# Attention in two bursts of three score blocks a turn, with PSUM banks shared out anew

## The chip, the cores and the metric

One core of a Trainium2 chip runs the whole program. The metric is the device time of one execution in microseconds, the median of the runs shown. Engines are named as the profile names them: PE (TensorE, matmuls), DVE (VectorE), ACT (ScalarE), POOL (GpSimd) and SP, which issues DMAs. Each takes its instructions in the order in which they stand in its queue.

## What is computed

Sigmoid attention for 4 batches of 12 heads (448 tokens, 64 wide), then two layers on its output:

```python
def _attn_ref(q, k, v):
    scores = scale * np.matmul(q, k.transpose(0, 1, 3, 2)) - np.log(S)
    attn = 1.0 / (1.0 + np.exp(-scores))
    return np.matmul(attn, v)

def _moe_ref(x, w_in, w_spatial, b_spatial, w_out):
    h = np.maximum(x @ w_in, 0.0)
    u, v = h[..., :512], h[..., 512:]
    v_n = (v - mean(v)) / np.sqrt(var(v) + 1e-06)
    v_s = np.einsum('ts,bsd->btd', w_spatial, v_n) + b_spatial[None, :, None]
    return (u * v_s) @ w_out

def _moe2_ref(x, g_ln, w_ch1, w_ch2):
    xn = normalised(x) * g_ln
    return x + np.maximum(xn @ w_ch1, 0.0) @ w_ch2
```

## The kernel before

Most products are made of three matmuls on operands split in two parts (`mm3`, lines 265 to 268: high x high, high x low, low x high). Attention fills the first 226 of 1063 us; the rest of the kernel is untouched by the change.

Attention works on pairs of heads, 24 in all, numbered p. A **turn** of the main loop (from line 815 on) handles pairs p and p+1; turn t has p = 2t. A pair's 448 key rows are three blocks of 128 (`scores`, six matmuls a block, line 416, two at a time on the two row halves of the array) and a rest of 64, which `scores_rest` (line 429) does for two pairs at once. Each block of scores goes into a double PSUM bank, from which ACT's sigmoid (line 403) writes SBUF. `sums` (line 456) multiplies a pair's three blocks with its values v, and `sums_rest` (line 443) adds the rest; `x_end` then writes the pair's columns of x, by a copy on ACT (line 303) and a subtraction on DVE (line 304). Where this text says **rests**, it means `scores_rest` of this turn's pairs, `sums_rest` of the turn before, and one `x_end`.

Ahead of a pair's scores its q and k are loaded by SP (four DMAs, lines 379 and 380) into rings of three, and split by `qk_split`: two casts on DVE (lines 395, 398) and, from pair 2 on, two subtractions on POOL (lines 399, 400). The split parts lie in rings of two, so the cast for pair p+2 waits for the scores of pair p.

Beside attention the first layer begins. Its weight w_in comes in eight **chunks**: chunks 0 to 3 for `hv`, 4 to 7 for `hu`. A chunk passes four steps: *load* (SP, line 277, 768 KB), *scale* (POOL, line 284), *bits* (three operations on DVE, lines 293, 294, 297) and *split* (a copy on ACT, line 303, and a subtraction on DVE, line 304). Raw chunks lie in a ring of two, so the load of chunk 3 waits for the bits of chunk 1. `W_IN_PLAN` says at which point of which turn a step is issued: "3A" is turn 3 behind its first burst of scores. The products (`hv`, a group of 18 matmuls with 512 columns; `hu`, 18 with 448) come from a generator that `Stream.run` advances by a budget of microseconds, `4 * BG_US` = 9.2 a turn; it yields None when an input isn't settled, that is when it wasn't written at least `LAG` = 1 step back. A group of 18 accumulates in one PSUM bank, is passed through Relu on ACT (lines 521, 550) and stored.

A turn before: the rests, scores of two blocks, sums of pair p-1, two blocks, sums of pair p, two blocks, products. The eight PSUM banks are four for two double banks (scores), two for products (`ps1`) and two for sums (`psa`). The engines' queues follow the program's order; nothing is reordered.

Of the kernel before, what the change touches and what calls it, by code (L numbers as in the profile page):

```python
# [16 lines left out]
P = 128  # L17
# [4 lines left out]
KC = DM // P  # L22
# [19 lines left out]
LAG = 1  # L42
# [16 lines left out]
    "5B": ["split 7"],  # L59
# [135 lines left out]
class Stream:  # L195
# [21 lines left out]
def sigmoid_attention_gmlp_mlp(ctx: ExitStack, tc, q, k, v, w_in, w_sp, w_out, g_ln, w1, w2, out):  # L217
# [6 lines left out]
    ps_a = ctx.enter_context(tc.tile_pool(name="ps_a", bufs=2, space=bass.MemoryType.PSUM))  # L224
# [25 lines left out]
    def psa():  # L250
        return ps_a.tile([P, 512], F32, tag="psa", name="psa")

    singles = [lambda: ps_1.tile([P, 512], F32, tag="ps1", name="ps1")]

    def ps1():
        singles.append(singles.pop(0))
        return singles[-1]()

    def ps2():
        return ps_s.tile([P, 2, 512], F32, tag="ps2", name="ps2")  # L260
# [12 lines left out]
    vu = dict(v=Ring(F, DH, 2), u=Ring(F, S, 2))  # L273
# [32 lines left out]
    class Chunk:  # L306


        def __init__(self, src, place):
            self.src, self.place, self.ready = src, place, None  # L310
# [42 lines left out]
    rv = Ring(F, 512, 4)  # L353
    af_r = Ring(F, 2 * S, 5)
# [7 lines left out]
    x_done = {}  # L362
# [71 lines left out]
    def sums_rest(p):  # L434
# [3 lines left out]
        pairs[p + 1]["ps"] = psa()  # L438
# [25 lines left out]
    def x_end(p):  # L464
# [6 lines left out]
        x_done[b, hp] = now[0]  # L471
# [32 lines left out]
    def hv(b):  # L504
# [4 lines left out]
        for c in range(NB2 // 2, NB2) if b % 2 else range(NB2 // 2):  # L509
            ps = ps1()  # L510
            cols = slice(c * P, (c + 1) * P)
            for kc in range(KC):
                while not settled(x_done.get((b, kc)), 1) or not all(
                    settled(t.ready) for t in wv_chunks[: -(-(kc + 1) * DH // WC)]
                ):
                    yield None
# [3 lines left out]
            vf = vu["v"].next().ap(DH)  # L520
# [6 lines left out]
            yield 3 * 0.216  # L527
# [8 lines left out]
    def hu(b):  # L536
# [278 lines left out]
    for p in range(0, n_pairs, 2):  # L815
        if p:
            rests(p)
        scores((p, 0), (p, 1))
        w_in_step(f"{p // 2}A")
# [3 lines left out]
        else:  # L823
            rests(p)
# [24 lines left out]
    now[0] += 1  # L849
# [4 lines left out]
    for r in a_rings:  # L854
        r.free()
# [158 lines left out]
```

## Time and profile before

| | us |
|---|---|
| three runs | 1064.35, 1065.24, 1065.28 (median 1065.24) |
| the profiled execution | 1065.46 |
| its span, first to last instruction | 1063.3 |
| PE busy in the span | 1055.5 (99%) |
| PEld, DVE, ACT, POOL busy | 914.0, 550.7, 298.2, 118.1 |

The durations below come from the profiled execution. In a timeline each line is a run of like instructions: its start, the time to the end of the last of them, engine, line, operation, and how many; what stands in brackets is idle time before it and what ended it. Matmuls overlap, so the pace of a run is read from the distance of starts. Where a matmul of two parts is one instruction in the program, the trace may count two (sums: six matmuls, x12).

### The profile page before, as it was taken

The page shows a single profiled execution, that of the slowest core. Times are in us where ns is not written, and L with a number is a line of the kernel's source. Part 1 is how long each engine was busy: PE and PEld are TensorE (multiplying, and loading weights), DVE is VectorE, ACT ScalarE, POOL GpSimd, SP SyncE. Part 2 cuts the span into 40 slices and gives each one's busy share as a digit, 9 for nine tenths or more (in the row PEclk, how much of TensorE's full clock was granted, in tenths as well). Part 3 has the DMA queues.
Part 4 walks back from the last instruction along what each step waited for, and adds up shares of the span by engine and source line. Part 5 has one row for each costly group of instructions (what it writes and reads, how often), then busy time and mean ns, then how long its engine had stood idle before and what let it go on. Part 6 is the DMA issues. An engine that isn't in the chain of part 4 may idle for free.

```text
span 1063.3 us, 14008 instructions
## 1 busy us (share of the span) xinstructions
PE 1055.5 (99%) x5812; PEld 914.0 (86%) x5812; DVE 550.7 (52%) x789; ACT 298.2 (28%) x445; POOL 118.1 (11%) x104
## 2 busy tenths in 40 slices
PE   8999999999999999999999999999999999999998
PEld 5556666679999999999989899998999898999988
DVE  3764131146757755463646465555646364645533
ACT  5754444434523421111212121211112121112100
POOL 4553211122134400000000000000000000000000
PEclk9999999999999999999999999999999999999999
DMA  8853336254301111010202111110202020111013
GB/s 219 239 171 101 126 110 178 82 193 130 138 1 59 62 60 60 25 65 30 90 30 73 47 60 60 60 60 30 72 18 89 30 90 30 60 60 60 1 60 149
DMA packets 31951, 87.15 MB, mean 82 GB/s; under 512 B 7568, under 2 KB 16016, under 8 KB 31760
## 3 DMA queue, kind: packets, MB, share of 16 engines
q1 hardware_dynamic: 29808, 78.23, 22.9%
q0 software_dynamic: 1600, 7.34, 2.0%
q8 instruction: 46, 0.75, 0.3%
q10 hardware_dynamic: 480, 0.69, 0.2%
q14 instruction: 17, 0.14, 0.0%
HBM read 73.38 MB, written 12.86 MB: 81 GB/s over the span
## 4 chain that ended last, share of the span: by engine, by line
PE 96%; DMA 1%; DVE 1%; issue 0%; POOL 0%; ACT 0%; ACTq 0%; DVEq 0%; SPq 0%
PE ps L266 22%; PE ps L268 22%; PE ps L267 22%; PE psa L268 6%; PE psa L267 6%; PE psa L266 6%; PE psa L456 5%; PE ps L416 4%; PE ps L429 1%; PE psa L443 1%; DMA f_all<-in_k 1%; PE psa L654 0%; PE ps L654 0%; DMA f_all<-in_w_in 0%; DMA f_all<-in_q 0%; DVE f_all L294 0%
## 5 line engine op out<-in xcount | busy, mean ns | idle before, releaser
L266 PE MATMUL ps<-r_all 128*128 128x384 f32 (+2 forms) x1250 | 435.8, 349 | 0.0
L268 PE MATMUL ps<-r_all 128*128 128x384 f32 (+2 forms) x1250 | 433.8, 347 | 0.0
L267 PE MATMUL ps<-r_all 128*128 128x384 f32 (+2 forms) x1250 | 433.6, 347 | 0.0
L266 PEld LDWEIGHTS ps<-r_all 128*128 128x128 f32 x1250 | 235.1, 188 | 17.8 <-issue 3.8
L267 PEld LDWEIGHTS ps<-r_all 128*128 128x128 f32 x1250 | 235.1, 188 | 14.1
L268 PEld LDWEIGHTS ps<-r_all 128*128 128x128 f32 x1250 | 234.9, 188 | 12.9
L709 DVE TENSOR_TENSOR f_all<-ps,f_all 128x768 f32<-128x768 f32 x168 | 160.4, 955 | 163.1 <-PE ps L268 163.1
L268 PE MATMUL psa<-r_all 128*128 128x512 f32 (+3 forms) x338 | 123.6, 366 | 0.0
L267 PE MATMUL psa<-r_all 128*128 128x512 f32 (+3 forms) x338 | 123.4, 365 | 0.0
L266 PE MATMUL psa<-r_all 128*128 128x512 f32 (+3 forms) x338 | 123.0, 364 | 0.0
L691 ACT ACTIVATE r_all<-psa 128x512 fp32r<-128x512 f32 (+1 forms) x48 | 26.0, 541 | 276.5 <-PE psa L268 276.5
L303 ACT CAST r_all<-f_all 128x768 fp32r<-128x768 f32 x60 | 49.9, 834 | 172.3 <-DVE f_all L297 138.6
L403 ACT ACTIVATE f_all<-ps,bias_s 128x896 f32<-128x896 f32 x84 | 80.8, 1005 | 44.6 <-PE ps L416 23.4
L692 DVE SCALAR_TENSOR_TENSOR r_all<-ps,r_all 128x512 fp32r<-128x512 f32 (+1 forms) x48 | 29.9, 623 | 90.6 <-ACT r_all L691 90.6
L268 PEld LDWEIGHTS psa<-r_all 128*128 128x128 f32 x338 | 63.7, 188 | 9.6
L304 DVE TENSOR_TENSOR r_all<-f_all,r_all 128x768 fp32r<-128x768 f32 x60 | 59.6, 994 | 23.6 <-ACT r_all L303 23.6
L267 PEld LDWEIGHTS psa<-r_all 128*128 128x128 f32 x338 | 63.6, 188 | 8.8
L266 PEld LDWEIGHTS psa<-r_all 128*128 128x128 f32 x338 | 63.7, 188 | 8.6
L416 PEld LDWEIGHTS ps<-r_all 64*128 64x128 f32 x432 | 37.7, 184 | 28.5 <-issue 17.4
L294 DVE SCALAR_TENSOR_TENSOR f_all<-f_all 128x768 uint32<-128x768 uint32 x60 | 60.6, 1009 | 2.1
L304 DVE TENSOR_TENSOR r_all<-psa,r_all 128x448 fp32r<-128x448 f32 (+1 forms) x38 | 22.6, 595 | 74.0 <-ACT r_all L303 73.9
L456 PE MATMUL psa<-f_all 128*64 128x448 f32 x288 | 59.6, 548 | 1.1 <-DVE r_all L304 1.1
(85 smaller groups left out, 673.8 us busy)
## 6 DMA issues: line engine op xcount, KB each, us to landing
f_all<-in_w SPq DMA_DIRECT2D x48, 768.0 KB, 4.2
f_all<-in_v SPq DMA_DIRECT2D x24, 256.0 KB, 3.8
f_all<-in_w_in SPq DMA_DIRECT2D x8, 768.0 KB, 5.2
f_all<-in_k SPq DMA_DIRECT2D x45, 112.0 KB, 3.6
f_all<-in_q SPq DMA_DIRECT2D x45, 112.0 KB, 3.7
out_y<-f_all SPq DMA_DIRECT2D x13, 384.0 KB, 2.3
vscr<-f_all SPq DMA_DIRECT2D x14, 256.0 KB, 2.0
uscr<-f_all SPq DMA_DIRECT2D x16, 224.0 KB, 1.9
```

The source lines that it names most:

```text
L266: nc.tensor.matmul(ps, lh, rh, start=first, stop=False)
L267: nc.tensor.matmul(ps, lh, rl, start=False, stop=False)
L268: nc.tensor.matmul(ps, ll, rh, start=False, stop=last)
L294: nc.vector.scalar_tensor_tensor(bits, low, 29, bits, op0=ALU.logical_shift_right, op1=ALU.bitwise_or)
L303: nc.scalar.copy(hi, x)
L304: eng.tensor_sub(lo, x, hi)
L403: nc.scalar.activation(af, ps[:, :, :S], AF.Sigmoid, bias=bias_s, scale=1.0 / math.sqrt(D))
L416: nc.tensor.matmul(ps[:, j, :S], a[w][rows, kc], a[x][rows], start=(i == 0), stop=(i == 2))
L456: nc.tensor.matmul(a["ps"][rows, :S], a["v"][:, 4 * j + c], af[:, j], start=(p % 2 == 0 and c == 0), stop=(p % 2 == 1 and c == 2),)
L691: nc.scalar.activation(hh[:, f], ps[:, :n], AF.Relu)
L692: nc.vector.scalar_tensor_tensor(hl[:, f], ps[:, :n], 0.0, hh[:, f], op0=ALU.max, op1=ALU.subtract)
L709: nc.vector.tensor_add(y[:, hs], ps, y[:, hs])
```

## The change

Scores go out in two bursts of three blocks a turn, pair by pair, where three bursts of two stood. A third double bank joins them (`ps_x`, for the time of attention); sums and products now share the two banks of `ps1`, and `psa` is gone. For that, products are issued in whole groups (`Stream.run` stops only where the yielded cost is not positive), and a group is begun only when all of its batch's x and all chunks of its weight have been issued; that they were issued a step back is no longer asked (`LAG` is gone). A turn is now: the rests, three blocks, sums of pair p-1, products, three blocks, sums of pair p. The casts for pair p+2 stand behind the first burst, the values of pair p+1 are loaded in the turn of pair p (a ring of three in place of four), and `W_IN_PLAN` names its points anew (A, B, C, D: behind the first burst, ahead of products, behind them, at the turn's end).

```diff
 W_IN_PLAN = {
-    "0B": ["scale 0"],
-    "1A": ["bits 0", "scale 1"],
-    "1B": ["split 0", "bits 1", "load 2"],
+    "0D": ["scale 0"],
+    "1A": ["bits 0"],
+    "1B": ["load 2", "scale 1"],
+    "1D": ["split 0", "bits 1"],
     "2A": ["split 1", "load 3", "scale 2"],
-    "2B": ["bits 2", "scale 3"],
+    "2D": ["bits 2", "scale 3"],
     "3A": ["split 2", "bits 3", "load 4"],
-    "3B": ["split 3", "load 5", "scale 4"],
-    "3C": ["bits 4", "scale 5"],
-    "4A": ["split 4", "bits 5", "load 6"],
-    "4B": ["split 5", "load 7", "scale 6"],
-    "4C": ["bits 6", "scale 7"],
-    "5A": ["split 6", "bits 7"],
-    "5B": ["split 7"],
+    "3B": ["split 3", "load 5", "scale 4", "bits 4"],
+    "3C": ["split 4", "load 6", "scale 5"],
+    "3D": ["bits 5"],
+    "4A": ["split 5", "load 7", "scale 6"],
+    "4B": ["bits 6", "scale 7"],
+    "4C": ["split 6"],
+    "4D": ["bits 7"],
+    "5A": ["split 7"],
 }
...
     def run(self, us):
         self.owed += us
-        while self.owed > 0 and not self.done:
-            try:
-                cost = next(self.gen)
-            except StopIteration:
+        cost = 0.0
+        while not self.done and (self.owed > 0 or cost > 0):
+            cost = next(self.gen, None)
+            if cost is None:
                 self.done = True
-                return
-            if cost is None:
+            elif cost == 0:
                 self.owed = 0.0
-                return
-            self.owed -= cost
+            else:
+                self.owed -= abs(cost)
...
-    ps_a = ctx.enter_context(tc.tile_pool(name="ps_a", bufs=2, space=bass.MemoryType.PSUM))
...
+    ps_x = att.enter_context(tc.tile_pool(name="ps_x", bufs=1, space=bass.MemoryType.PSUM))
+    doubles += [double(ps_s), double(ps_x)]
...
-    rv = Ring(F, 512, 4)
-    af_r = Ring(F, 2 * S, 5)
+    rv = Ring(F, 512, 3)
+    af_r = Ring(F, 2 * S, 6)
...
-        pairs[p + 1]["ps"] = psa()
+        pairs[p + 1]["ps"] = ps1()
...
         for c in range(NB2 // 2, NB2) if b % 2 else range(NB2 // 2):
+            while (b, KC - 1) not in x_done or not wv_chunks[-1].ready:
+                yield 0
             ps = ps1()
             cols = slice(c * P, (c + 1) * P)
             for kc in range(KC):
-                while not settled(x_done.get((b, kc)), 1) or not all(
-                    settled(t.ready) for t in wv_chunks[: -(-(kc + 1) * DH // WC)]
-                ):
-                    yield None
...
     for p in range(0, n_pairs, 2):
+        turn = p // 2
         if p:
             rests(p)
-        scores((p, 0), (p, 1))
-        w_in_step(f"{p // 2}A")
+        scores((p, 0), (p, 1), (p, 2))
+        if not p:
+            rests(p)
+        qk_split(p + 2)
+        w_in_step(f"{turn}A")
         if p:
             sums(p - 1)
             x_end(p - 1)
-        else:
-            rests(p)
         qk_load(p + 3)
         if not p:
             wv_chunks[1].load()
-        beside()
         qk_load(p + 4)
+        if p:
+            pv_load(p + 1)
         pv_load(p + 2)
-        pv_load(p + 3)
...
-        scores((p, 2), (p + 1, 0))
-        beside()
+        beside(f"{turn}B")
+        bg.run(4 * BG_US)
+        beside(f"{turn}C")
+        scores((p + 1, 0), (p + 1, 1), (p + 1, 2))
+        qk_split(p + 3)
+        beside("")
         sums(p)
-        qk_split(p + 2)
-        w_in_step(f"{p // 2}B")
-        beside()
-        scores((p + 1, 1), (p + 1, 2))
-        qk_split(p + 3)
-        beside()
-        bg.run(4 * BG_US)
-        w_in_step(f"{p // 2}C")
+        beside(f"{turn}D")
```

The order on three engines, before and now. A name with a number (ps_444) is one PSUM tile; "x6" counts like instructions; r_all and f_all are the two SBUF arenas; lines of the changed kernel are some two to five higher (416 is 418, 429 is 431, 443 is 445, 456 is 458, 403 is 405, 303 is 308, 304 is 309, 395 and 398 are 397 and 400, 266 to 268 are 271 to 273).

PE in turn 3, from the rests to the first products, before:

```order
L429 MATMUL ps_431<-f_all 64x448 x4
L443 MATMUL psa<-f_all 64x448 x4
L416 MATMUL ps_444<-r_all 128x448 x6
L416 MATMUL ps_452<-r_all 128x448 x6
L456 MATMUL psa<-f_all 64x448 x6
L416 MATMUL ps_484<-r_all 128x448 x6
L416 MATMUL ps_492<-r_all 128x448 x6
L456 MATMUL psa<-f_all 64x448 x6
L416 MATMUL ps_515<-r_all 128x448 x6
L416 MATMUL ps_523<-r_all 128x448 x6
L266 MATMUL ps_215<-r_all 128x512
L267 MATMUL ps_215<-r_all 128x512
```

and now:

```order
L431 MATMUL ps_420<-f_all 64x448 x4
L445 MATMUL ps_409<-f_all 64x448 x2
L445 MATMUL ps_426<-f_all 64x448 x2
L418 MATMUL ps_433<-r_all 128x448 x6
L418 MATMUL ps_441<-r_all 128x448 x6
L418 MATMUL ps_449<-r_all 128x448 x6
L458 MATMUL ps_426<-f_all 64x448 x6
L271 MATMUL ps_492<-r_all 128x512
L272 MATMUL ps_492<-r_all 128x512
L273 MATMUL ps_492<-r_all 128x512
```

The three bursts of two blocks are two of three, and products stand between them, right behind the sums; in the changed kernel 54 product matmuls stand there in a row, where 45 stood at the turn's end before. Over all turns, products stand in ten turns before (turns 1, 2, 3 and 5 to 11) and in eight now (3 and 5 to 11).

DVE in turn 1, from a pair's end to the bits of chunk 1, before:

```order
L304 TENSOR_TENSOR r_all<-psa,r_all 128x448
L293 TENSOR_SCALAR f_all<-f_all 128x768
L294 SCALAR_TENSOR_TENSOR f_all<-f_all 128x768
L297 SCALAR_TENSOR_TENSOR f_all<-f_all 128x768
L304 TENSOR_TENSOR r_all<-psa,r_all 128x448
L395 CAST r_all<-f_all 128x384
L398 CAST r_all<-f_all 128x448
L304 TENSOR_TENSOR r_all<-f_all,r_all 128x768
L293 TENSOR_SCALAR f_all<-f_all 128x768
L294 SCALAR_TENSOR_TENSOR f_all<-f_all 128x768
L297 SCALAR_TENSOR_TENSOR f_all<-f_all 128x768
```

and now, from the casts for pair 4:

```order
L397 CAST r_all<-f_all 128x384
L400 CAST r_all<-f_all 128x448
L298 TENSOR_SCALAR f_all<-f_all 128x768
L299 SCALAR_TENSOR_TENSOR f_all<-f_all 128x768
L302 SCALAR_TENSOR_TENSOR f_all<-f_all 128x768
L309 TENSOR_TENSOR r_all<-ps_220,r_all 128x448
L397 CAST r_all<-f_all 128x384
L400 CAST r_all<-f_all 128x448
L309 TENSOR_TENSOR r_all<-f_all,r_all 128x768
L298 TENSOR_SCALAR f_all<-f_all 128x768
L299 SCALAR_TENSOR_TENSOR f_all<-f_all 128x768
L302 SCALAR_TENSOR_TENSOR f_all<-f_all 128x768
```

The first three operations of lines 293 to 297 (now 298 to 302) are the bits of chunk 0, the second three those of chunk 1. Both moved back: the casts of a pair stand ahead of each, and the second also stands behind the casts for pair 5, which wait for the turn's second burst.

ACT in turn 4, from the first block's sigmoid to the sigmoid of the next rests, before:

```order
L403 ACTIVATE f_all<-ps_614,bias_s 128x896
L403 ACTIVATE f_all<-ps_622,bias_s 128x896
L303 CAST r_all<-f_all 128x768
L303 CAST r_all<-psa 128x448
L403 ACTIVATE f_all<-ps_654,bias_s 128x896
L403 ACTIVATE f_all<-ps_662,bias_s 128x896
L303 CAST r_all<-f_all 128x768
L403 ACTIVATE f_all<-ps_685,bias_s 128x896
L403 ACTIVATE f_all<-ps_693,bias_s 128x896
L403 ACTIVATE f_all<-ps_709,bias_s 128x896
```

and now:

```order
L405 ACTIVATE f_all<-ps_619,bias_s 128x896
L405 ACTIVATE f_all<-ps_627,bias_s 128x896
L405 ACTIVATE f_all<-ps_635,bias_s 128x896
L308 CAST r_all<-f_all 128x768
L308 CAST r_all<-ps_612 128x448
L308 CAST r_all<-f_all 128x768
L405 ACTIVATE f_all<-ps_675,bias_s 128x896
L405 ACTIVATE f_all<-ps_683,bias_s 128x896
L405 ACTIVATE f_all<-ps_691,bias_s 128x896
L405 ACTIVATE f_all<-ps_713,bias_s 128x896
```

Now the copy of split 6 (the last CAST from f_all) stands ahead of all three sigmoids of the turn's second burst (ps_675 to ps_691); before, the turn's last copy (split 5) stood ahead of the last two.

## Rows read from the trace of the kernel before

**Rows 1.** The page, busy time by engine and the granted clock in 40 slices.

```profile
PE 1055.5 (99%) x5812; PEld 914.0 (86%) x5812; DVE 550.7 (52%) x789; ACT 298.2 (28%) x445; POOL 118.1 (11%) x104
...
PEclk9999999999999999999999999999999999999999
```

**Rows 2.** Timeline of PE, turn 6: start, us, engine, line, tiles, count, idle before.

```profile
96.44 0.37 PE L268 MATMUL ps<-r_all 128*128 128x448 f32 x1
96.73 0.98 PE L429 MATMUL ps<-f_all 64*64 64x448 f32 x8
...
98.40 1.48 PE L416 MATMUL ps<-r_all 64*128 64x448 f32 x12
99.80 2.48 PE L456 MATMUL psa<-f_all 128*64 128x448 f32 x12
102.21 1.49 PE L416 MATMUL ps<-r_all 64*128 64x448 f32 x12
...
107.46 0.47 PE L266 MATMUL ps<-r_all 128*128 128x448 f32 x1
107.77 0.36 PE L267 MATMUL ps<-r_all 128*128 128x448 f32 x1
107.97 0.37 PE L268 MATMUL ps<-r_all 128*128 128x448 f32 x1
```

**Rows 3.** Timeline of PE, the start of turn 1.

```profile
16.01 2.18 PE L429 MATMUL ps<-f_all 64*64 64x448 f32 x7 [0.49 <-DMA f_all<-in_k]
...
19.25 1.49 PE L416 MATMUL ps<-r_all 64*128 64x448 f32 x12
```

**Rows 4.** Timeline of PE, the rests and sums of turn 5.

```profile
74.00 1.16 PE L429 MATMUL ps<-f_all 64*64 64x448 f32 x8 [0.49 <-ACT f_all L403]
...
79.68 1.48 PE L416 MATMUL ps<-r_all 64*128 64x448 f32 x12
82.21 2.65 PE L456 MATMUL psa<-f_all 128*64 128x448 f32 x12 [1.05 <-DVE r_all L304]
```

**Rows 5.** Timeline of all engines, 26 to 36 us: SP's loads and DVE.

```profile
26.53 4.06 SPq L277 DMA_DIRECT2D f_all<-in_w_in  x2
...
29.24 0.96 DVE L297 SCALAR_TENSOR_TENSOR f_all<-f_all 128x768 uint32<-128x768 uint32 x1
...
35.86 0.54 SPq L385 DMA_DIRECT2D f_all<-in_v  x1
```

**Rows 6.** DMA issues from 30 to 38 us, with median us to landing.

```profile
f_all<-in_v SPq DMA_DIRECT2D x2, 256.0 KB, 4.3
```

**Rows 7.** Timeline of all engines, turn 3 before its products.

```profile
43.22 1.48 PE L416 MATMUL ps<-r_all 64*128 64x448 f32 x12
...
44.20 1.91 ACT L403 ACTIVATE f_all<-ps,bias_s 128x896 f32<-128x896 f32 x2
...
46.86 0.96 DVE L304 TENSOR_TENSOR r_all<-f_all,r_all 128x768 fp32r<-128x768 f32 x1 [2.08 <-ACT r_all L303]
...
47.73 0.55 DVE L293 TENSOR_SCALAR f_all<-f_all 128x768 uint32<-128x768 uint32 x1
...
49.31 0.96 DVE L297 SCALAR_TENSOR_TENSOR f_all<-f_all 128x768 uint32<-128x768 uint32 x1
...
51.30 1.77 DVE L304 TENSOR_TENSOR r_all<-f_all,r_all 128x768 fp32r<-128x768 f32 x1
```

**Rows 8.** Timeline of all engines, the chain of chunk 6 in turns 4 and 5.

```profile
72.31 1.03 POOL L399 TENSOR_TENSOR r_all<-f_all,r_all 128x384 fp32r<-128x384 f32 x1 [11.74 <-DVE r_all L395]
...
75.13 2.31 POOL L284 TENSOR_SCALAR f_all<-f_all 128x768 f32<-128x768 f32 x1
...
77.47 1.35 DVE L293 TENSOR_SCALAR f_all<-f_all 128x768 uint32<-128x768 uint32 x1 [1.08 <-POOL f_all L284]
...
80.66 0.96 DVE L297 SCALAR_TENSOR_TENSOR f_all<-f_all 128x768 uint32<-128x768 uint32 x1
...
81.66 0.83 ACT L303 CAST r_all<-f_all 128x768 fp32r<-128x768 f32 x1 [2.92 <-DVE f_all L297]
```

More of the change, by code (lines that the diff above doesn't have):

```diff
@@ L248, in sigmoid_attention_gmlp_mlp, with single, double, turned @@
     ctx.enter_context(tc.manual_schedule())
-    def psa():
-        return ps_a.tile([P, 512], F32, tag="psa", name="psa")
-    singles = [lambda: ps_1.tile([P, 512], F32, tag="ps1", name="ps1")]
+    def single(pool):
+        return lambda: pool.tile([P, 512], F32, tag="ps1", name="ps1")
+    def double(pool):
+        return lambda: pool.tile([P, 2, 512], F32, tag="ps2", name="ps2")
+    def turned(kinds):
+        kinds.append(kinds.pop(0))
+        return kinds[-1]()
+    singles, doubles = [single(ps_1)], [double(ps_s)]
     def ps1():
-        singles.append(singles.pop(0))
-        return singles[-1]()
+        return turned(singles)
     def ps2():
-        return ps_s.tile([P, 2, 512], F32, tag="ps2", name="ps2")
+        return turned(doubles)
     def wide():
@@ L272, in sigmoid_attention_gmlp_mlp @@
     dec_r = Ring(F, WC, 2)
-    vu = dict(v=Ring(F, DH, 2), u=Ring(F, S, 2))
+    vu = Ring(F, DH, 3)
     def w_load(src):
@@ L309, in __init__ @@
         def __init__(self, src, place):
-            self.src, self.place, self.ready = src, place, None
+            self.src, self.place, self.ready = src, place, False
         def load(self):
@@ L327, in split @@
             split(self.hi, self.lo, self.f)
-            self.ready = now[0]
+            self.ready = True
     def row_chunks(src, n, parts):
@@ L339, in idle @@
         pass
-    now = [0]
-    def settled(t, lag=LAG):
-        return t is not None and now[0] - t >= lag
+    att = ExitStack()
+    ps_x = att.enter_context(tc.tile_pool(name="ps_x", bufs=1, space=bass.MemoryType.PSUM))
+    doubles += [double(ps_s), double(ps_x)]
     wv = [R.alloc(KC * DH), R.alloc(KC * DH)]
@@ L361, in sigmoid_attention_gmlp_mlp @@
     pairs = {}
-    x_done = {}
+    x_done = set()
     def x_of(b):
@@ L450, in sums @@
         if p % 2 == 0:
-            a["ps"] = psa()
+            a["ps"] = ps1()
         for c in range(3):
@@ L470, in x_end @@
         split(xh, xl, pairs.pop(p)["ps"][:, :S])
-        x_done[b, hp] = now[0]
+        x_done.add((b, hp))
     def power(rs, var, half):
@@ L526, in hv @@
             nc.vector.bn_aggr(vraws[:, pr, c], st)
-            yield 3 * 0.216
+            yield -3 * 0.216
         if b % 2:
@@ L539, in hu @@
         wh, wl = (t.ap(KC, DH) for t in wu)
-        while not all(settled(t.ready) for t in wu_chunks):
-            yield None
+        while not wu_chunks[-1].ready:
+            yield 0
         for f in range(NDC):
@@ L798, in sigmoid_attention_gmlp_mlp, with beside @@
     step = iter(range(10**9))
-    def beside():
-        i = now[0] = next(step)
+    def beside(name):
+        w_in_step(name)
         jobs.pop(2)
-        if i == WO_FROM:
+        if next(step) == WO_FROM:
             c0, c1, c2, c3 = wo_chunks
@@ L836, in sigmoid_attention_gmlp_mlp @@
             nc.sync.dma_start(wsp_raw.ap(5 * S), w_sp)
-        scores((p, 2), (p + 1, 0))
-        beside()
-        sums(p)
-        qk_split(p + 2)
-        w_in_step(f"{p // 2}B")
-        beside()
-        scores((p + 1, 1), (p + 1, 2))
-        qk_split(p + 3)
-        beside()
-        bg.run(4 * BG_US)
-        w_in_step(f"{p // 2}C")
+        beside(f"{turn}B")
[4 more added lines that the diff above has]
+        beside("")
+        sums(p)
+        beside(f"{turn}D")
     rests(n_pairs)
-    now[0] += 1
     sums(n_pairs - 1)
     x_end(n_pairs - 1)
-    singles.append(psa)
-    now[0] = 10**9
     for r in a_rings:
         r.free()
+    att.close()
+    del doubles[1:]
+    ps_b = ctx.enter_context(tc.tile_pool(name="ps_b", bufs=2, space=bass.MemoryType.PSUM))
+    singles.append(single(ps_b))
     wsp_b = R.at(PLACE_WSP, 8 * S)
@@ L921, in sigmoid_attention_gmlp_mlp @@
     free_all(xp)
-    vu["v"].free()
-    vu["u"].free()
+    vu.free()
     for b in range(B):
```

7 lines of the change are left out of this document (3 added, 4 removed).

## The prediction

> **What bounds the kernel now.** I read the page's busy line first: PE is busy for 99% of the span [rows 1]. The granted clock stands at full in all forty slices, so no stretch runs at the lower level [rows 1]. That leaves two things in attention by which the same matmuls can take less or more time: what PE loses where one kind of matmul follows another, and what it loses in waits. I read the first from PE's timeline of an undisturbed turn, turn 6 [rows 2], and the second from the few rows that carry a wait in brackets [rows 3, 4]. Then I read the queues that feed PE in the turns in which chunks of w_in are loaded and split: SP's loads and their landing [rows 5, 6], and the operations of DVE, ACT and POOL around the splits [rows 7, 8].
>
> **What a burst costs.** In turn 6 two product matmuls of 448 columns start 0.20 us apart (107.77 and 107.97). The second of a group follows its first only after 0.31 us (107.46 to 107.77), and the rests follow the last after 0.29 us (96.44 to 96.73) [rows 2]. So a group of products costs about 0.11 on entering and 0.09 on leaving. A burst of two blocks of scores is six steps (two row halves run together) and takes 1.40 us (98.40 to 99.80) [rows 2]: six steps of 0.20, and again 0.20 for entering and leaving. A burst of three blocks is then nine steps and 0.20: 2.00 us. Sums take 2.41 us (99.80 to 102.21), the rests with their sums 1.67 us (96.73 to 98.40) [rows 2].
>
> **What the change removes.** Three bursts a turn become two: 3 x 1.40 - 2 x 2.00 = 0.20 us a turn. In turn 0 it is worth nothing: turn 1 starts when pair 3's k has landed (the wait at 16.01), so PE begins the scores of turn 1 at 19.25 in both kernels [rows 3]. Eleven turns remain: 2.2 us. Products stood in ten of the turns before and stand in eight now (turns 1 and 2 had short pieces): two groups less, 0.4 us. Together **-2.6 us**. Two waits of before lie around turns 4 and 5: 0.49 us at 74.00, for a score bank; and sums that should follow the burst at 79.68 at 81.08 start at 82.21, 1.13 us late [rows 4]. That is **-1.6 us**, if nothing takes their place: the third double bank removes the first, and the second hangs on the bits of a chunk, which the new plan puts elsewhere.
>
> **What it adds: three waits of PE.** A turn without products is now 1.67 + 2 x 2.00 + 2 x 2.41 = 10.49 us. Turn 2 starts at 19.25 + 8.82 = 28.07, turn 3 at 38.56, if nothing waits. Everything on PE is in order, so behind a wait nothing goes ahead. Three chains end behind PE:
>
> First, **the values of pair 5 at the start of turn 3.** Their load moved from turn 1 to turn 2 and stands on SP behind the load of chunk 3 and eight loads of q and k. The load of chunk 3 waits for the bits of chunk 1, which moved from the middle to the end of turn 1, behind its second burst. That burst starts at 19.25 + 2.00 + 2.41 = 23.66; its sigmoids start 0.98 us after it and take 0.955 each (44.20: 1.91 for two, after the burst at 43.22) [rows 7], so three end at 27.5; on ACT follows the copy of split 0 (0.83 [rows 8]), on DVE its subtraction and then the bits. The subtraction takes 0.96 alone (46.86) and 1.77 beside POOL (51.30) [rows 7]; bits take 2.54 alone (47.73 to 49.31 + 0.96) [rows 7] and 4.15 beside POOL (77.47 to 80.66 + 0.96) [rows 8]. So the bits end between 31.8 and 34.3; I take 32.8, nearer to the rows without POOL, which has pauses there. In the kernel before these bits ended at 29.24 + 0.96 = 30.20, SP was through with the load at 26.53 + 4.06 = 30.59 and issued values at 35.86 [rows 5]; values take 4.3 us to land in that stretch [rows 6]. So they land 0.4 + 5.3 + 4.3 = 10.0 us after the bits, at 42.8 (41.8 to 44.3). The rests' sums want them three quarters into the rests: 38.56 + 1.25 = 39.8. Wait: **3.0 us** (2.0 to 4.5).
>
> Second, **products of turn 3 on chunk 3.** The condition that held products off until a split lay a step back is gone, and turn 3 issues three whole groups right behind its sums. In the turn before, split 3 ended on DVE at 51.30 + 1.77 = 53.07, 9.85 us after that turn's first burst (43.22) [rows 7]. Now ACT does a third sigmoid ahead of the copy of split 2 (+0.955), and the bits of chunk 3 stand behind that: 10.8. PE wants chunk 3 in the fifth of six steps of its first group: 2.00 + 2.41 + 0.11 and 13 matmuls of 512 columns at 0.20 x 512/448 = 0.23, so 7.5 us after the burst. Wait: **3.3 us**; 2.5 with the subtraction at 0.96, 4.9 with the bits beside POOL (+1.61).
>
> Third, **the rests of turn 5.** With three double banks they need the bank of the first block of turn 4's second burst, so its sigmoid. On ACT that sigmoid now stands behind the copy of split 6, which waits for the bits of chunk 6, these for POOL's scale, and that for POOL's two subtractions for pair 10, which begin after the first burst of turn 4. From that burst's start: 2.00; 0.5 until POOL starts (an estimate: last matmul's end and cast); 2.3 for two subtractions (2.82 from 72.31 to 75.13, where DVE worked beside them); 2.31 for the scale; 4.15 for the bits, since POOL goes on to the scale of chunk 7; 0.83; 0.96 [rows 7, 8]. That is 13.05, where PE is through with burst, sums, burst and sums after 8.82. Wait: **4.2 us**. With bits at 2.54: 2.6. With POOL's 2.82 and a scale 0.8 longer: 5.5. For this chain speaks that it is the one behind the wait at 82.21, where the bits ended at 81.6 [rows 4, 8].
>
> **What moves at no cost.** The casts for pair p+2 follow the first burst; most of a turn lies between them and their use. Sums now share two banks with products: the first group needs the bank that x_end gives back during the first burst and the sums (4.41 us); if that cover is short, the wait falls into those above. Sigmoids of a turn with products (seven, 6.7 us) fit beside it.
>
> **The sum.** -2.6 - 1.6 + 3.0 + 3.3 + 4.2 = +6.3 us on the execution of 1065.46 us (span 1063.3, the rest lies around it): 1071.8. That execution lies 0.2 above the median of 1065.24, so the forecast is **1071.5 us**. With all three waits at their low ends 2.0 + 2.5 + 2.6 - 4.2 = +2.9, 1068.1; at their high ends 4.5 + 4.9 + 5.5 - 4.2 = +10.7, 1076.
>
> **Rivals.** *The clock falls in the new waits.* The 1.13 us before 82.21 left the clock up [rows 1, 4]; the new waits are three to four times that. If PE came back at the lower level, rests and burst behind a wait (3.67 us) would take twice as long: 1075.2 with one such wait, 1078.9 with two. The Trainium skill, "TensorE: Matmul & The Clock Gate", section "HAM oscillation — how this bites in real kernels", says that waits of 3 to 5 us between short bursts bring the clock down each time. No row here shows a fall, so it gets 0.17.
>
> *Only the third wait is there.* The first two end behind DVE's bits. If DVE works ahead (it idled 2.08 us before 46.86 [rows 7]), values and chunk 3 come in time and only the last is paid: -4.2 + 4.2, **1065.2 us**, not slower. It decides if the bits of chunk 1 end before 29.8. Against it: sigmoids and the copy on ACT alone put them past 31.8. 0.14.
>
> *None is there.* Then -4.2: **1061.0 us**, faster. The copy of split 6 would have to come before the second burst of turn 4 has ended, 4 us sooner than its chain on POOL and DVE allows. 0.09.
>
> **Chances and range.** The forecast holds 0.60. Within 0.2% (2.1 us, about what a measurement of this kernel can tell from no change) lies the case of one wait: same 0.14; faster 0.09; slower 0.60 + 0.17 = 0.77. The range leaves out the case without waits, most of the one-wait case, and the upper part of the clock's: 1066.5 to 1077.5.
>
> **What would show it.** On PE, bursts of 2.00 us and sums of 2.41 in undisturbed turns; waits at the rests' sums of turn 3 (on the values' DMA), in the first products (on the split) and at the rests of turn 5 (on the sigmoid), of 3.0, 3.3 and 4.2 us; the two of before gone; the granted clock below full behind them if the first rival holds. I am wrong in the mechanism if PE's waits add up to under 4 us, and in a size if one of the three is out of its bounds.

## The result, and the profile after

The changed kernel takes **1076.01 us** in the median (1074.57 to 1078.18), the kernel before 1065.26: a ratio of 1.0105, with a 95% interval of 1.0087 to 1.0123. It is slower, by 10.7 us. The profiled execution is the shortest of four, 1074.57 us (span 1072.5); against that of before (1065.46, span 1063.3) the difference to explain is 9.1 us. From the last products behind attention on (410 matmuls, 82.84 us) the two traces are alike, and turn 1 starts at 19.22 where it started at 19.25 [rows 3]; so all of it lies between.

The page answers to [rows 1] with this line, and with the same digit in all forty slices of the granted clock:

```profile
PE 1056.3 (98%) x5812; PEld 916.6 (85%) x5812; DVE 551.0 (51%) x789; ACT 296.9 (28%) x445; POOL 117.6 (11%) x104
```

That hides the matter: PE's busy time grew by 0.8 us only, and a slice of the clock is 27 us long. PE's waits by line (line, releaser, us in total, times, longest) say more:

```profile
PE ps L431 <- ACT f_all L405: 3.8, 1, 3.8
PE ps L431 <- DMA f_all<-in_q: 3.4, 2, 1.9
PE ps L271 <- ACT r_all L308: 2.4, 1, 2.4
...
```

One of the two waits on in_q (1.9) is the old one at the start of turn 1. The others, with two short ones that stand in the brackets below, are the three waits of the forecast. The first, at the start of turn 3, on PE's timeline (start, us, engine, line, tiles, count, idle before), with SP's queue below it:

```profile
38.58 0.96 PE L431 MATMUL ps<-f_all 64*64 64x448 f32 x2
41.05 1.41 PE L431 MATMUL ps<-f_all 64*64 64x448 f32 x5 [1.51 <-DMA f_all<-in_q]
...
43.99 0.97 PE L445 MATMUL ps<-f_all 64*64 64x448 f32 x4 [1.15 <-DMA f_all<-in_v]
44.89 2.09 PE L418 MATMUL ps<-r_all 64*128 64x448 f32 x18
```

```profile
27.76 6.53 SPq L282 DMA_DIRECT2D f_all<-in_w_in  x2
...
40.42 0.89 SPq L387 DMA_DIRECT2D f_all<-in_v  x2
```

The rests with their sums last from 38.58 to 44.89, 6.31 us where an undisturbed turn has 1.66 to 1.67 [rows 2]: **+4.65**. SP stands at the load of chunk 3 until 34.29, then issues eight loads and, at 40.42, the values.

The second, in turn 3's first product group, and the third, between turns 4 and 5, with ACT's rows there:

```profile
49.32 0.50 PE L271 MATMUL ps<-r_all 128*128 128x512 f32 x1
...
54.77 0.50 PE L271 MATMUL ps<-r_all 128*128 128x512 f32 x1 [2.44 <-ACT r_all L308]
55.76 0.50 PE L272 MATMUL ps<-r_all 128*128 128x512 f32 x1 [0.49 <-DVE r_all L309]
...
65.32 2.11 PE L418 MATMUL ps<-r_all 64*128 64x448 f32 x18
```

```profile
77.87 2.48 PE L458 MATMUL ps<-f_all 128*64 128x448 f32 x12
84.10 1.81 PE L431 MATMUL ps<-f_all 64*64 64x448 f32 x8 [3.76 <-ACT f_all L405]
...
87.33 2.48 PE L418 MATMUL ps<-r_all 64*128 64x448 f32 x18
89.74 2.48 PE L458 MATMUL ps<-f_all 128*64 128x448 f32 x12
```

```profile
82.31 0.83 ACT L308 CAST r_all<-f_all 128x768 fp32r<-128x768 f32 x1 [5.81 <-DVE f_all L302]
83.05 3.90 ACT L405 ACTIVATE f_all<-ps,bias_s 128x896 f32<-128x896 f32 x4
```

The 54 products of turn 3 take 16.0 us (49.32 to 65.32); the same 54 take 12.48 undisturbed (in a kernel below), so **+3.5**. From sums to rests it is 84.10 - 77.87 = 6.23 us where sums take 2.41: **+3.8**. Rests and burst behind that wait take 3.23 and 2.41 us (to 87.33, to 89.74), where 1.66 and 2.02 are usual: **+2.0**. The reason stands in the row of that stretch (window, span, busy us and count of PE, PEld, DVE, ACT and POOL, granted clock, DMA share, GB/s):

```profile
42.00:70.00 28.00, 23.92 (x129) 15.26 (x130) 19.75 (x27) 11.53 (x15) 13.29 (x9) 1.00 0.59 179
70.00:90.00 20.00, 16.24 (x112) 9.00 (x106) 14.54 (x18) 11.87 (x15) 10.21 (x7) 0.91 0.51 141
```

0.91 over 20 us: by that row the clock stood for some 3.6 us (an estimate: 1.8 us lost, at half speed) at 1.2 in place of 2.4 GHz. No other stretch of attention is below 1.00. Against these stand the two old waits, gone from their places [rows 4] (-2.0 with the slower starts behind them), and bursts and product groups (-2.6 as forecast; undisturbed bursts of three take 2.01 to 2.04). Together 4.65 + 3.5 + 3.8 + 2.0 - 2.0 - 2.6 = +9.4, for 9.1 measured.

The other three executions were 1.3 to 3.6 us longer than the profiled one. Their mean granted clocks are 0.995, 0.992 and 0.993, the profiled one's is 0.998; before it was 1.000.

### The profile page after: what moved, and what is told of

It is laid out like the page before. It is cut to its first block, busy times and chain, and to the rows that moved or that the text cites. A ratio compares the mean times of both kernels' runs of the same rounds, so it can differ in the third digit from the quotient of the medians.

```text
span 1072.5 us, 13998 instructions
## 1 busy us (share of the span) xinstructions
PE 1056.3 (98%) x5812; PEld 916.6 (85%) x5812; DVE 551.0 (51%) x789; ACT 296.9 (28%) x445; POOL 117.6 (11%) x104
## 4 chain that ended last, share of the span: by engine, by line
PE 94%; DMA 2%; DVE 2%; issue 1%; ACT 0%; POOL 0%; SPq 0%; ACTq 0%; POOLq 0%; DVEq 0%
PE ps L271 28%; PE ps L272 28%; PE ps L273 28%; PE ps L458 4%; PE ps L418 3%; DMA f_all<-in_k 2%; PE ps L431 1%; PE ps L654 1%; PE ps L445 1%; DVE f_all L299 0%; DVE r_all L309 0%; DMA f_all<-in_q 0%; DVE f_all L302 0%; DMA f_all<-in_v 0%; PE ps L593 0%
## 5 line engine op out<-in xcount | busy, mean ns | idle before, releaser
L271 PE MATMUL ps<-r_all 128*128 128x384 f32 (+3 forms) x1588 | 558.7, 352 | 2.4 <-ACT r_all L308 2.4
L272 PE MATMUL ps<-r_all 128*128 128x384 f32 (+3 forms) x1588 | 557.0, 351 | 0.5 <-DVE r_all L309 0.5
L273 PE MATMUL ps<-r_all 128*128 128x384 f32 (+3 forms) x1588 | 557.3, 351 | 0.0
L271 PEld LDWEIGHTS ps<-r_all 128*128 128x128 f32 x1588 | 298.7, 188 | 31.8 <-issue 5.6
L272 PEld LDWEIGHTS ps<-r_all 128*128 128x128 f32 x1588 | 298.7, 188 | 23.6 <-DVE r_all L309 0.8
L273 PEld LDWEIGHTS ps<-r_all 128*128 128x128 f32 x1588 | 298.6, 188 | 22.5
L709 DVE TENSOR_TENSOR f_all<-ps,f_all 128x768 f32<-128x768 f32 (+1 forms) x169 | 161.0, 953 | 163.3 <-PE ps L273 163.2
L691 ACT ACTIVATE r_all<-ps 128x512 fp32r<-128x512 f32 (+1 forms) x96 | 52.0, 542 | 394.1 <-PE ps L273 394.1
L692 DVE SCALAR_TENSOR_TENSOR r_all<-ps,r_all 128x512 fp32r<-128x512 f32 (+1 forms) x96 | 59.7, 622 | 144.9 <-ACT r_all L691 144.9
L299 DVE SCALAR_TENSOR_TENSOR f_all<-f_all 128x768 uint32<-128x768 uint32 x60 | 60.8, 1013 | 2.1
L302 DVE SCALAR_TENSOR_TENSOR f_all<-f_all 128x768 uint32<-128x768 uint32 x60 | 59.2, 987 | 2.1
L458 PE MATMUL ps<-f_all 128*64 128x448 f32 x288 | 59.4, 548 | 0.0
L418 PE MATMUL ps<-r_all 64*128 64x448 f32 x432 | 51.4, 377 | 0.2
L291 ACT ACTIVATE f_all<-f_all 128x768 f32<-128x768 f32 x52 | 46.9, 905 | 0.0
L298 DVE TENSOR_SCALAR f_all<-f_all 128x768 uint32<-128x768 uint32 x60 | 37.2, 619 | 3.3 <-ACT f_all L291 1.8
```

Of the source, the lines that this page charges most:

```text
L271: nc.tensor.matmul(ps, lh, rh, start=first, stop=False)
L272: nc.tensor.matmul(ps, lh, rl, start=False, stop=False)
L273: nc.tensor.matmul(ps, ll, rh, start=False, stop=last)
L299: nc.vector.scalar_tensor_tensor(bits, low, 29, bits, op0=ALU.logical_shift_right, op1=ALU.bitwise_or)
L302: nc.vector.scalar_tensor_tensor(bits, high, 0x80000000, bits, op0=ALU.bitwise_and, op1=ALU.bitwise_or)
L418: nc.tensor.matmul(ps[:, j, :S], a[w][rows, kc], a[x][rows], start=(i == 0), stop=(i == 2))
```

## The experiments

Each kernel is the changed one with the edit shown, unless said otherwise. Ratios are against the kernel before, on the same chip. Differences between profiles may be between chips; the median of the kernel before lay between 1064.7 and 1065.3 us on all of them.

### The load of chunk 3 behind the loads of its turn

```diff
-    "2A": ["split 1", "load 3", "scale 2"],
+    "2A": ["split 1", "scale 2"],
+    "2B": ["load 3"],
```

> The changed kernel, with one step moved: the load of chunk 3 is issued in turn 2 behind the loads of q, k and values of that turn, no longer ahead of them. Theory: the 4.65 us by which the rests and their sums of turn 3 lasted too long (6.31 us where an undisturbed turn has 1.66) come from SP, which held eight loads and the values behind the load of chunk 3 until the bits of chunk 1 had ended. They then go out from about 28 us on, land by 39, and turn 3 takes up its rests at 38.6 with 1.66 us. The wait for chunk 3 in turn 3's products (3.5 us) is counted from that turn's first burst and stays: 1074.6 - 4.65 = 1069.9 us beside the profiled execution of the changed kernel, 1071.3 beside its median of 1076.0. Rival A: the transfers themselves are slow in that stretch, whoever stands ahead of them; then the wait stays, 1076. Rival B: chunk 3 is late by its load and not by the burst; then products wait 4.65 us longer, 8.1 in all, and the time stays at 1076.

Measured: 1073.04 us, ratio 1.0076 (1.0061 to 1.0092); profiled 1072.35. On PE, POOL and DVE of turn 3:

```profile
37.63 0.98 PE L432 MATMUL ps<-f_all 64*64 64x448 f32 x8
...
39.29 2.09 PE L419 MATMUL ps<-r_all 64*128 64x448 f32 x18
...
50.98 0.79 PE L272 MATMUL ps<-r_all 128*128 128x512 f32 x1 [4.24 <-ACT r_all L309]
...
63.27 2.12 PE L419 MATMUL ps<-r_all 64*128 64x448 f32 x18
```

```profile
42.28 2.90 POOL L290 TENSOR_SCALAR f_all<-f_all 128x768 f32<-128x768 f32 x1 [1.00 <-ACT f_all L406]
...
45.22 1.37 DVE L299 TENSOR_SCALAR f_all<-f_all 128x768 uint32<-128x768 uint32 x1
...
48.42 1.65 DVE L303 SCALAR_TENSOR_TENSOR f_all<-f_all 128x768 uint32<-128x768 uint32 x1
```

The first operation of the same bits in the changed kernel:

```profile
50.74 0.55 DVE L298 TENSOR_SCALAR f_all<-f_all 128x768 uint32<-128x768 uint32 x1
```

The first wait is gone, to the hundredth: 39.29 - 37.63 = 1.66 us. SP's place in the queue was its cause, and rival A falls. But rival B holds in part. The 54 products now take 19.56 us (43.71 to 63.27), 7.1 too long in place of 3.5: 5.2 around two waits, and 1.6 at the low clock behind them. In the changed kernel split 3 ended 10.8 us after the turn's first burst began, here 12.6 (50.97 + 0.96 - 39.29). The load goes out at 36.2, 3.1 us ahead of that burst and not 11, and the scale begins 3.0 us behind the burst's start, where it began 0.3 ahead of it. Yet the bits begin 5.9 us behind that start in both kernels, when DVE is through with split 2 (45.22 here, 50.74 there). It is the bits that last longer, 4.85 us where they had 3.1: POOL is done with its scale only at 45.18 and does its two subtractions and then its next scale beside them; the subtractions had ended at 50.01 in the changed kernel, ahead of the bits. So the late load costs its time through POOL and DVE. The first of the two waits is 4.24 instead of 2.44, and the clock falls with it (0.88 between 42 and 70 us). Of 4.65 us won, some 3.5 are given back in the same turn.

### The bits of chunk 3 ahead of split 2

```diff
-    "3A": ["split 2", "bits 3", "load 4"],
+    "3A": ["bits 3", "split 2", "load 4"],
```

> The changed kernel, with two steps swapped: the bits of chunk 3 stand ahead of the split of chunk 2 on DVE in turn 3. Theory: products of turn 3 wait because the bits of chunk 3 stand behind the subtraction of split 2, this behind the copy on ACT, and that behind three sigmoids. DVE idled 1.37 us there and the subtraction took 1.40; bits now begin about 2.5 us sooner, split 3 ends about 2.5 us sooner, and the wait of 3.5 us shrinks to about 1.0: 1072.1 beside the profiled execution, 1073.5 beside the median. Rival: chunk 2 becomes late in place of chunk 3 (its split now stands behind the bits), products wait as long on it, and the time stays at 1076.

Measured: 1071.44 us, ratio 1.0060 (1.0042 to 1.0079); profiled 1070.88. Turn 3's products take 14.72 us, 2.2 too long in place of 3.5, with two waits of 0.85 and 0.81 for the two splits: the rival holds for the first of them, as chunk 2 is late now too. Split 3 ends 9.6 us after the first burst (44.26 to 52.52 + 1.31). I had expected about 1.0 for what is left: the bits, now beside POOL's subtractions, took 4.2 us. The mechanism holds, its gain was 1.3 and not 2.5.

More came from a place that the edit does not touch. The third wait is the same as ever, and here the clock stayed up behind it:

```profile
82.21 1.29 PE L431 MATMUL ps<-f_all 64*64 64x448 f32 x8 [3.76 <-ACT f_all L405]
...
84.17 2.12 PE L418 MATMUL ps<-r_all 64*128 64x448 f32 x18
86.22 2.48 PE L458 MATMUL ps<-f_all 128*64 128x448 f32 x12
```

```profile
70.00:90.00 20.00, 16.24 (x111) 9.24 (x110) 14.38 (x20) 13.30 (x18) 11.75 (x8) 1.00 0.55 155
```

Rests and burst take 1.96 and 2.05 us where they took 3.23 and 2.41. So 1.6 of the 3.7 us between the two profiles are the clock.

### Split 6 behind the second burst of turn 4

```diff
-    "4C": ["split 6"],
-    "4D": ["bits 7"],
+    "4D": ["split 6", "bits 7"],
```

> The changed kernel, with one step moved: the split of chunk 6 is issued in turn 4 behind the second burst, its sigmoids and its sums, no longer ahead of that burst. Theory: the rests of turn 5 waited 3.8 us for a sigmoid that stood on ACT behind the copy of split 6, and the clock fell in that wait, which cost another 2.0 us (rests and burst behind it 5.64 us where undisturbed ones take 3.68). Both go: 1074.6 - 5.8 = 1068.8 beside the profiled execution, 1070.2 beside the median, granted clock 1.00 between 70 and 90 us. The two waits of turn 3 stay at 4.65 and 3.5. Rival A: the clock falls for what came before, not for this wait; then 2.0 us stay: 1070.8 and 1072.2, clock 0.91 there. Rival B: chunk 7, whose bits stand behind split 6, comes late to the products of turn 5, and that wait takes back what was won.

Measured: 1070.54 us, ratio 1.0051 (1.0036 to 1.0066); profiled 1069.87. The wait of 3.8 us is gone and with it the fall of the clock there, so rival A falls. Something of rival B's kind comes in its place, one turn on:

```profile
79.92 0.92 PE L444 MATMUL ps<-f_all 64*64 64x448 f32 x4
81.00 0.97 PE L444 MATMUL ps<-f_all 64*64 64x448 f32 x4 [0.16 <-DMA f_all<-in_v]
...
87.40 0.47 PE L270 MATMUL ps<-r_all 128*128 128x448 f32 x1 [1.02 <-DVE r_all L308]
```

```profile
42.00:70.00 28.00, 25.47 (x134) 16.45 (x130) 17.46 (x25) 10.38 (x14) 11.76 (x7) 0.94 0.53 166
70.00:90.00 20.00, 18.82 (x123) 10.23 (x120) 15.64 (x21) 14.16 (x18) 12.26 (x8) 1.00 0.69 185
```

Between 79.92 and 87.40 some 2.2 us are lost: 1.1 in the rests' sums, 1.1 ahead of the products. For the latter DVE is named; its operation that ends there is the subtraction of `x_end`, which stands behind the bits of chunk 7. That operation gives back the bank that sums and products now share. The clock fell in turn 3 instead (0.94), where it had not in the changed kernel. Of the 4.7 us between the two profiles 3.6 are won between turns 4 and 5, 1.2 are lost again in the products of turn 3, and 2.1 have nothing to do with the edit: turn 1 began at 17.09 in place of 19.22 us.

### All three

> The changed kernel with all three edits: load of chunk 3 behind the loads of turn 2, bits of chunk 3 ahead of split 2, split of chunk 6 behind the second burst of turn 4. Theory: the three waits are separate and their gains add: 4.65 + 2.5 + 5.8 = 12.9 us, so 1061.6 us, which is faster than the kernel before (1065.2) by 3.6; what is left of it is the gain of bursts of three (2.6) and of two old waits (2.0) less about 1 us of the wait for chunk 3. Rival: they aren't separate; a turn that starts 4.65 us sooner finds its chunks as much less ready, so most of the first gain comes back as waits in turns 3 to 5, and the time is 1065 or more.

Measured: 1069.24 us (1065.55 to 1072.21), ratio 1.0041 (1.0029 to 1.0054); profiled 1072.21, the longest of ten. My theory of separate gains (1061.6) falls, and the rival (1065 or more) holds. Rests of turn 3 take 1.66 us, and the wait of 3.8 is gone, but:

```profile
45.30 2.56 POOL L289 TENSOR_SCALAR f_all<-f_all 128x768 f32<-128x768 f32 x1 [0.96 <-DMA f_all<-in_w_in]
```

```profile
48.39 1.37 DVE L298 TENSOR_SCALAR f_all<-f_all 128x768 uint32<-128x768 uint32 x1
```

```profile
53.50 0.50 PE L272 MATMUL ps<-r_all 128*128 128x512 f32 x1 [2.58 <-DVE r_all L309]
...
55.27 0.50 PE L272 MATMUL ps<-r_all 128*128 128x512 f32 x1 [0.80 <-DVE r_all L309]
```

```profile
19.00:28.00 9.00, 9.00 (x42) 4.63 (x39) 4.23 (x6) 4.98 (x6) 6.25 (x6) 0.64 0.69 184
```

With the turns closer together POOL's scale of chunk 3 waits for its load and ends at 47.86. DVE, which has no pause from 42.31 on, first in the bits of chunk 2, comes to those of chunk 3 at 48.39: 4.5 us behind the burst's start, where it came 2.8 behind it with these bits moved alone. So the products of turn 3 are still 5.6 us too long, 3.4 in waits and 1.6 at the low clock. The profiled execution also began late: turn 1 starts at 20.82, where it waited for the first q and k, 1.6 us behind the changed kernel's, and PE came back at the low clock (0.64 between 19 and 28 us), which cost 2.1 us more.

### Products a turn later

The single edits took 3.0, 4.6 and 5.5 us off the changed kernel's median, all three together 6.8 of the 10.7. So the waits can be mended only in part by moving single steps: the plan gives a chunk too little time between its steps in turns 2 to 4. This kernel has the changed one's bursts and banks, and another plan; products begin a turn later, and from turn 6 on more of them are asked for a turn:

```diff
     "1D": ["split 0", "bits 1"],
-    "2A": ["split 1", "load 3", "scale 2"],
+    "2A": ["split 1", "scale 2"],
+    "2B": ["load 3"],
     "2D": ["bits 2", "scale 3"],
-    "3A": ["split 2", "bits 3", "load 4"],
-    "3B": ["split 3", "load 5", "scale 4", "bits 4"],
-    "3C": ["split 4", "load 6", "scale 5"],
-    "3D": ["bits 5"],
-    "4A": ["split 5", "load 7", "scale 6"],
-    "4B": ["bits 6", "scale 7"],
-    "4C": ["split 6"],
-    "4D": ["bits 7"],
-    "5A": ["split 7"],
+    "3A": ["split 2"],
+    "3B": ["load 4", "bits 3"],
+    "3D": ["scale 4"],
+    "4A": ["split 3", "load 5", "scale 5"],
+    "4B": ["bits 4"],
+    "4C": ["split 4", "bits 5", "load 6", "scale 6"],
+    "4D": ["split 5", "load 7", "scale 7"],
+    "5B": ["bits 6"],
+    "5D": ["bits 7"],
+    "6A": ["split 6", "split 7"],
...
-        bg.run(4 * BG_US)
+        bg.run((6 if turn > 5 else 4) * BG_US)
```

> The changed kernel with its bursts and banks, and another plan for w_in: products begin in turn 4 and not in turn 3, loads of chunks stand behind the loads of q, k and values of their turn, each bits and each split has most of a turn after what it waits for, and no copy of a split stands on ACT ahead of scores whose sigmoids it could hold. Turns 3 and 5 then have no products, and turns from 6 on take somewhat more of them (13.8 us asked for in place of 9.2). Theory: the three waits are a matter of the plan alone; without them the bursts and the third double bank leave 1065.2 - 2.6 (bursts, groups) - 2.0 (the two old waits) = 1060.6 us, less up to 0.8 for fewer groups of products; granted clock 1.00 in all of attention. Turn 3 lasts 10.5 us from its rests to the rests of turn 4. Rival: two banks shared by sums and products, or a late chunk, hold PE in turn 4 or 6 instead, for 2 us or more; then 1063 or above. If the kernel ends at 1065 or above with no wait above 0.5 us on PE, bursts of three are not worth what I took them for.

Measured: **1060.87 us** (1059.70 to 1061.45), ratio 0.9960 (0.9946 to 0.9975): faster than both kernels. Against the kernel before on the same chip (1064.73) it is 3.9 us less, where 4.6 to 5.4 were expected. All four executions have a mean granted clock of 1.000. Of PE's waits one of 0.35 us is left between turn 1 and the end of attention. It stands ahead of the last matmul of turn 6's first group, for the subtraction of split 7, which ends at 92.94; the next group then starts 0.3 us late, for the bank that `x_end` gives back at 93.47. The two cost 0.8 us. Turn 3, which has no products, then the 54 products and that wait:

```profile
38.52 0.98 PE L433 MATMUL ps<-f_all 64*64 64x448 f32 x8
...
40.19 2.09 PE L420 MATMUL ps<-r_all 64*128 64x448 f32 x18
42.21 2.48 PE L460 MATMUL ps<-f_all 128*64 128x448 f32 x12
...
49.03 0.98 PE L433 MATMUL ps<-f_all 64*64 64x448 f32 x8
...
55.12 0.50 PE L273 MATMUL ps<-r_all 128*128 128x512 f32 x1
...
67.60 2.11 PE L420 MATMUL ps<-r_all 64*128 64x448 f32 x18
...
93.00 0.47 PE L275 MATMUL ps<-r_all 128*128 128x448 f32 x1 [0.35 <-DVE r_all L311]
```

10.5 us from rests to rests, as the prediction had it for a turn without products (10.49), with bursts of 2.02. The 54 products take 12.48 us (55.12 to 67.60). This settles that the loss lay in the waits and that they came from the plan, with the turns in which products stand: bursts and banks are the same in both kernels, which are 15 us apart in their medians.

### Five waits put in

In the changed kernel the first sigmoid of a turn's second burst is written several times over, which holds the next rests:

```diff
+AGAIN = {(13, 0): 8, (15, 0): 5, (17, 0): 8, (19, 0): 5, (21, 0): 8}
...
-            a["a", c] = sigmoid(af_r.next().ap(2, S), ps)
+            af = af_r.next().ap(2, S)
+            for _ in range(AGAIN.get((p, c), 1)):
+                a["a", c] = sigmoid(af, ps)
```

> The changed kernel with five waits of PE put into turns that have none: the first sigmoid of the second burst is repeated on ACT (the same values written again), seven times more in turns 6, 8 and 10, four times more in turns 7 and 9. One such sigmoid takes 0.935 us behind another, and the rests of the next turn need its bank 4.43 us after the burst began, when the first would have ended at 1.94. So rests wait 4.05 us three times and 1.25 us twice: 14.7 us more than the changed kernel if waits cost only their length (1089.3 beside its profile, 1090.7 beside its median). Theory, the clock falls in a wait of PE of about 4 us: rests and burst behind each of the three long ones take up to 2 us more, 6 in all, so 1095 to 1097; behind the short ones nothing. Rival: a wait of 4 us alone does not bring the clock down, it needs what stood before it in turns 3 and 4 (turns without products, other waits); then the clock is 1.00 from 110 us on, and the time is 1089 to 1091.

Measured: 1100.38 us, ratio 1.0336 (1.0319 to 1.0353); profiled 1099.61. The first long wait:

```profile
128.36 2.48 PE L461 MATMUL ps<-f_all 128*64 128x448 f32 x12
135.64 1.68 PE L434 MATMUL ps<-f_all 64*64 64x448 f32 x8 [4.80 <-ACT f_all L406]
...
138.73 2.48 PE L419 MATMUL ps<-r_all 64*128 64x448 f32 x18
141.15 2.48 PE L461 MATMUL ps<-f_all 128*64 128x448 f32 x12
```

ACT's eleven sigmoids there, eight of them to the same tile, take 11.06 us, 1.005 each and not 0.935, so the long waits are 4.9 us, the short ones 1.75, and not 4.05 and 1.25; that puts the time above the 1095 to 1097 expected. Rows of the stretches with the first long wait and the first short one:

```profile
131.00:145.00 14.00, 9.36 (x52) 5.52 (x53) 1.91 (x4) 11.10 (x13) 2.33 (x3) 0.88 0.31 86
...
153.00:172.00 19.00, 17.32 (x107) 11.88 (x104) 3.12 (x8) 11.86 (x14) 4.35 (x4) 1.00 0.59 174
```

The clock fell with each long wait (0.88, 0.85 and 0.94 in their stretches) and in neither short one. Behind the long ones rests and burst were 1.8, 2.9 and 1.5 us too long, behind the short ones 0.2 and 0.3. Waits 18.1 and what followed 6.7 make 24.8, of the 25.0 between this profile and the changed kernel's. The rival falls: turns of full work stood around these waits, and nothing that the others had before them was needed. They were, though, about 1 us longer than the third wait of the changed kernel.

### Two double banks in place of three

In the kernel with products a turn later, the third double bank is left unused:

```diff
-    ps_x = att.enter_context(tc.tile_pool(name="ps_x", bufs=1, space=bass.MemoryType.PSUM))
-    doubles += [double(ps_s), double(ps_x)]
+    doubles += [double(ps_s)]
```

> The kernel with products from turn 4 on and the later plan for w_in, with one part of the change undone: two double banks for scores in place of three (the third stays unused); bursts are still of three blocks. Theory: the third bank is what a burst of three needs. With two, the third block needs the bank of the first, so its sigmoid, which ends 1.94 us after the burst began (it starts at 0.98 and takes 0.955), where the block could begin at 1.33: 0.6 us a burst, in 23 bursts 14 us, so about 1075 us (1060.9 for the kernel with three). Bursts then last 2.6 us in place of 2.0. Rival: sigmoids keep up, as a burst of two had the same two banks, and nothing changes: 1061.

Measured: 1076.40 us, ratio 1.0104 (1.0075 to 1.0133), of two executions; 15.5 us more than with three, and 11.2 more than the kernel before.

```profile
30.15 1.48 PE L419 MATMUL ps<-r_all 64*128 64x448 f32 x12
32.18 0.88 PE L419 MATMUL ps<-r_all 64*128 64x448 f32 x6 [0.56 <-ACT f_all L406]
32.99 2.48 PE L459 MATMUL ps<-f_all 128*64 128x448 f32 x12
```

The third block waits for the sigmoid of the first, here 0.56 us, 24 times and 12.9 us in all, and this burst takes 2.84 us: 0.82 more, not 0.6. The wait was foreseen; that its price is a third higher was not. The bursts' gain rests on the third double bank.

## Why the prediction was right, and where its sizes were off

The forecast was 1071.5 us with a range of 1066.5 to 1077.5; 1076.0 came out. Slower was right, and for the reasons named; the size was short by 4.5 us. The figure lies where the sum of all three waits at their high ends lay (1076), but it did not come about so: one wait of three was above its high end, and a fall of the clock came on top.

**What bounds the kernel, what a burst costs.** Right. Undisturbed bursts take 2.02 (forecast 2.00), sums 2.41, turns 2 and 3 start at 28.07 and 38.58 (forecast 28.07 and 38.56).

**What it removes.** Right. Two old waits were worth 2.0 and not 1.6: PE also starts slowly behind a wait. Bursts and groups at -2.6 fit the balance. The kernel with products a turn later comes near the sum of both, 4.6 us: it is 3.9 us faster than the kernel before on its chip, with 0.8 us lost in turn 6 and 0.3 in a burst of turn 5.

**First wait: 3.0 forecast, 4.65 measured,** above the high end of 4.5. Of the three waits this is the one most off. The bits of chunk 1 ended at 33.9 and not 32.8, since the subtraction before them (1.75) and the first of them (1.51) ran beside POOL's subtractions; eight loads and the step to the values took 6.1 us on SP and not 5.3; landing took 3.5 and not 4.3. That makes 1.2. The rest, 0.5, is the form of the wait: q and k of pair 7 also came late, PE worked in pieces, and what followed the wait ran slower. I had priced the wait by the landing alone.

**Second wait: 3.3 forecast, 3.5 measured.** The chain counted from the burst gave 10.8 us, and split 3 ended 54.75 + 0.96 - 44.89 = 10.8 after it. That the two agree so well is in part luck: against the kernel before, the subtraction of split 2 took 0.4 us more (1.40) and the bits 0.6 more (3.1), both beside POOL, and the subtraction of split 3 took 0.8 less (0.96). It also holds only because the first wait had delayed the burst. Without that wait the bits run beside POOL's subtractions, split 3 ends at 12.6, and the case is the one that the prediction priced at 4.9 us.

**Third wait: 4.2 forecast, 3.8 measured.** The chain is as described; bits took 3.2 us (79.07 to 82.28) where I took 4.15, since POOL had a scale to do beside them and not subtractions. They began 0.5 us later than reckoned, since the scale took about 2.9 us and not 2.31, which took back half of that.

**The rivals.** "The clock falls" was no alternative to the forecast but came on top of it: one fall in the profiled execution, for 2.0 us, where I had reckoned 3.7 (all of rests and burst at half speed; the clock was back before they ended). Giving it a chance of 0.17 and nothing in the sum was the failed step: three waits of 3 to 4 us were forecast, and each stood to lose a part of 2 us. The rival's own figure for one fall, 1075.2, came nearest, with the fall priced 1.7 us too high and the first wait 1.65 too low. The lower clocks of the other executions suggest that there it fell more often; where, those records don't tell. "Only the third wait" and "none" did not come, and the bits of chunk 1 ended 4 us past the point from which they would have.

**At no cost.** Banks shared by sums and products cost nothing in the changed kernel, as stated. They do once the third wait is gone: 1.1 us ahead of the products of turn 5.

Added up on the profiled executions, forecast less measured: first wait -1.65, second -0.2, third +0.4, clock -2.0, old waits +0.4, so -3.05, of -2.8 (1071.8 against 1074.6).

## What to carry to other kernels

A larger burst saves switches, but it also moves every buffer's release and every queue's order; price each wait that this can open by its chain, and expect that mending one lets the next appear, since the chain behind it was covered by the first. The cure was to give all steps a turn more, not to reorder one. A wait of PE costs its length and some 0.2 to 0.5 us of slow start; seven of eight waits of 3.8 to 4.8 us here cost 1.5 to 3 us beyond their length, with the low clock, so the sum should hold that as a term and not as a rival.

## What the hardware showed that was not expected

- **The clock behind a wait is not settled by its length alone.** Of eight waits of 3.76 to 4.8 us in these profiles, seven brought the clock from 2.4 to 1.2 GHz; one of 3.76 us, at the same place of the program, did not (1.00, in the kernel with the bits of chunk 3 first). Shorter ones in a row did too: 2.58 and 0.80 us (all three edits), and 2.04 and 0.49 (split 6 behind), each with a clock of 0.94 over the 28 us around, while 2.44 and 0.49 in the changed kernel left it at 1.00. The Trainium skill, "TensorE: Matmul & The Clock Gate", section "HAM oscillation — how this bites in real kernels", has waits of 3 to 5 us between short bursts bring it down each time; seven of the eight here agree, the eighth does not. What decides stays open. The clock is a part of the spread, 1065.55 to 1072.21 us in ten executions of one kernel with waits against 1059.70 to 1061.45 in four of the one without, but not the whole of it: executions of 1065.55 and 1070.58 us had the same mean clock, 0.998.
- **A wait costs more than its length at full clock too.** 1.75 us cost 1.95 to 2.1, and the 3.8 us that left the clock at 1.00 cost 4.2. In a burst a wait of 0.56 us cost 0.82, but there the bracket counts from the modelled end of the matmul before.
- **The start varies.** Turn 1 begins when the first q and k have landed, between 17.1 and 20.8 us in the profiles of kernels with the same instructions up to there; in the latest, the clock had fallen too.
